# A top-k attention block with a squared-ReLU feed-forward: first scores in parts, fewer reciprocals, other warming products, a new plan

## The chip, the cores and the metric

The program runs on one core of a Trainium2 chip. The core has five instruction streams, which run side by side and meet only at semaphores: TensorE (PE, matrix products; its weight loads are shown apart, as PEld), VectorE (DVE), ScalarE (ACT), GpSimd (POOL) and SyncE (SP, which issues most DMAs). The metric is the device time of one execution in microseconds (us), lower is better.

## The reference, cut to what matters

```python
# q, k, v: [8, 8, 576, 64] f32; w_in: [512, 2048], w_out: [2048, 512]
scores = (1 / sqrt(64)) * q @ k.T                   # per batch and head: 576 x 576
kth = the 32nd largest of each row
scores = where(scores >= kth, scores, -1e9)
attn = softmax(scores)
x = (attn @ v), heads side by side, as [4608, 512]
out = (max(x @ w_in, 0) ** 2) @ w_out
```

## The kernel before, in words

Two heads of one batch are a pair; a pair's 576 queries are cut into four blocks of 128 and one of 64 (two pairs share the blocks of 64). A block of one pair is a group, 144 groups in all, numbered n in the order of work. Every group goes through the same steps:

- Loads: `load_pair` brings q and k of the pair (three DMAs each) and v. `load_first` does it for the first pair alone, in smaller pieces: half of k over ACT's queue, the rest over SP's, q in two row blocks and a remainder.
- Transposes on PE (line 714) into two PSUM banks, copied to SBUF by ACT and DVE (lines 772 to 783, 848 to 850).
- `score`: four f32 products of PE (line 711; each shows as two passes), named by RUNS: run 0 is head 0, columns 384 to 575; run 1 head 1, columns 192 to 575; run 2 head 0, columns 0 to 383; run 3 head 1, columns 0 to 191. Head 0 lies in partitions 0 to 63, head 1 in 64 to 127. Runs 0 and 3 write the same PSUM bank, so run 3 waits on a semaphore, `fence`, that run 0 raises. One set of three banks holds the scores, so the next group's scores wait until these are read.
- `copied` (line 895): ACT copies the scores to SBUF. For the first two groups (`early`) a first quarter of the columns goes first and the rest after DVE's three folds.
- `top_k`: DVE folds the quarters of a row on each other (line 966, maxima), either itself or with POOL (lines 983 and 986, or 961 with a DMA of line 971 called edge) forms the rest, and finds the 32nd largest by rounds of the eight largest (lines 1019, 1024, 1034) and their replacement (line 1031). The third round's replacement is done by DVE (line 999) or by signs on ACT (line 1005) and a product on POOL (line 1009); the string SIGNS chooses, m or s, for each group.
- `attend`: ACT forms the mask (line 1053), PE transposes the scores with the mask added (line 714 and `steep_bf`), ACT takes the exponential (line 1110), PE multiplies with v (`fetch`).
- `gather` and `collect`: the sums are copied; for two pairs at a time DVE takes the reciprocals of the row sums (line 1184), POOL multiplies (line 1186), and a transposing DMA (line 1201) writes the result as the feed-forward's input.
- `feed`: PE multiplies with w_in, ACT takes the ReLU, POOL or ACT squares, PE multiplies with w_out (line 711).

The order of all this is planned in Python when the program is built. Every operation has a planned duration; the plan simulates the engines and gives each engine a fixed order. The strings in ORDERS hold that order (each character picks the next operation out of those left). On the chip an engine runs its instructions in that order and waits on semaphores, not on the plan's times. Besides, the planner puts in products that compute nothing needed, to keep PE at work: warming products at the start (`times`, 128 x 512 on `ones_bf`) and spare ones later. A warming product is placed only if PE is free at that planned time, the next planned operation is not delayed and one of two PSUM banks is free; otherwise it is dropped.

Of the kernel before, what the change touches and what calls it, by code (L numbers as in the profile page):

```python
# [448 lines left out]
def bass_top_k_attn__then__act_relu_squared_kernel(  # L449
# [24 lines left out]
    def sb(name, shape, dt=FP32, n=None):  # L474
        if n is None:
# [12 lines left out]
    SIGNS = "sssmmsmsssmmsmsmmsmssmsmmsmsmssmmmssssmsmmsmmsmmsmsmsmmsmsmsmsmmssmmsssmsmssmmsmmmsmmsssmmsmmmssmsmmsmsmssmsmsmmsmsmmmmmmmmmssmmmssmsmsmssmmmmmm"  # L488
# [7 lines left out]
    WARM = 6.4  # L496
    HOT = 6
# [8 lines left out]
            "222020343040402504406700Q561ON61714N6M1561W6H15T61Q71b461ZY75166AABB86618576B8A8158861968AC961EK6DHF176FAC6617"  # L506
            "5qs1q617B5A7186788991996DAC1C6B81b75A1X6BAD1B571868L56A1UAHHR1GGDHH519C8D6C1B9335491555867761686666156C8CABD77"
            "6196~118D8199568716=71;AAEEJJ1UU6MM15EQUUQ15655I9BA9148995744851AAgCf1CEONGF1IWIEGED1HQQIPP1QQLTT4C11J3251211G"
            "388964D1F7742G1444F55A14455A14D6AAB173445A51D597691666461kl61B5666615599666B1A7775716Z68J15C7S61CPA6861649UU1H"
            "HE9F1EGGE4FF17D8A46414925A55E155AA55155A67C18C96677415~119671A699771646A;A16CC61EEEJJO1NPPMRR14K5444454F4413F3"  # L510
            "E4554SCST1FCOFNKJR1GHEOE1JCDIL1HHMOHN4MMOOCG121H34J3275111864FB421G6444G1B4444551C5665A1D6665A1D56B6A1A7764AA1"
            "688DD61KQKP61IOOM1QmQN4544514544644FF464S4D1RHDQO1DMLHRHH1ELDFCD1HHOJHH4LMC165614M3111Q28I751P21233Q1K3333331O"
            "3333M122333775H14I633D1F393A616AF377421FB55551H445555144475o5914757Bh1H9f7694E1NEFE3DV1DEJDDPLL1CCDCCDCCPCG1OG"
# [16 lines left out]
        "dve": (  # L530
            "00330L0LJ0330FTSGFG0ENFM0LEEJ330GRIBQFH0LF4481BU8E10011O04c8J7I5667F7D1661L0MM98Z94AH5A8F1160O8M9L68WWJ7811046"
            "5N555962250EE4E54B55M9K2K2Y1H2G52F4D5552523102G3D4364OBO181702244DFD44524L270J7G86E2D8RQ24294281860GFG14656191"
            "812I2H05235354A951L160J51X442436C491A81706HH22T5465B52A2430H7G3F4U45R4B6PO59bA9A92H923S1SE26BN5A6992I231R735DB"
            "6A5990G9A41D1S029A6A5797A16E71705A5A67K7I777262660A9AM9K99958992C20A01888L88J8944171606A9A589867G7177D1S0C9C9C"
            "L9KD9YJ5H2H230Q4CPDN5BZ555252GS14555AB608481616062A9P999N995I19190D24BBB5A658297270A39999595972H20063CC3549547"
            "7576165155088888888574171D0D3A59A9AM9A91A1302C75A59758L72J25054E64C6Q5B62A273136F4E4D65CN5M6282712G354CD4OO5AB"
            "M2K281266SF78OEC3B2AAHCB2F55C2C1ALA0A5G8FF5E8EQDP27C2D09II96A5F8RQ92D2600J7I75G6678D1B1N0999KIAA558181A0AN5N89"
            "8J6872T2F0D5C55BAB658F2827B1B39OAONB9Ca5201G048D1D3D5E61841605E3CD65N59A5A82G2F0E3T74BB4AMAA5J0I191G22S03B5A4A"
            "4B64151D0C6C3AB4949J4A1615C70BA2AO9A9A551G1808C4C5ABMA597H88298C2RC309AM6A8B85HGA7272615805I7I6G6F76D871Q1A0OM"
            "A57JA7BG46171P0B5MB95867881ED1D05NC695898A9D2C2R0359898985727E2E61B5BA69999A5292C1B3A069NA85781H15064C5B5B5562"  # L540
            "J2505EF64C4C659N92K2J162G6U04RED555144171504ED23RB6AN4AM9188Y1Y0HkF8EF3D2N5B525K27370D3CDC6B5C552G7D271A028888"
            "889481C1A01847777476I171E03C55A6A95861J61G04EE64P5BN5556272505ED4CC4M5B59A929231C629A9A9A9B9294DCD2B129996L58J"
            "JJ79H2H2F1P4NDM66KCB62B291D3BC4ABA6A0HGA242C60AAAAAA59AA52C2C1A0A2MA8A8479F16170B1B9B9LB55716170D5BCBP5A59L752"
            "72G04FR4F65OEB652CJ2313U4CE4B4A5NA2829J12F9E2S4QD6BN2692416HG4T06RE74O5bAMM5952U2460Q74D5MB5AA55A828D2B13A9A96"
            "A95F82200584777M777K716180D2D4BC6ABK591G1906C72BAMBLCKA3C924F230B4MALL59JA9BV9GA52C2B1A2AJ9IBY595927C26186N770"
            "YL66HJ8GA1G1H03LB5AJ69FH518140O9BMDML958572G2E076C6AMA69IJ2Y2G1406CC56578572J2G0F54DD054548414F1E04D63A394M989"
            "8A17180B1B1QB9PBM6516170HFS84F8CM4BL5242303FT546DA59BK2J2B1X6014C164Q7dO884713140G3E3QD4C6cC5A59AA161D0DA29B68"
            "KB57G292D0PC4NC5MC5567268251S59A9A9L9K55II2I27R1EFE476B7J051E1706A3999999AFA52D2D029B9B557A7A26261658677706666"
            "667171AA0999O9598J95H191F0D4PC5NCBML65KJ92A2T04D50N6NAAMA1I1AV13EF30EC75EA575B2E2D06BB6B89A9B92E2813BA0A9OA955"
            "K9729728D16C76B9KB7CI272W1DED50Q4CAC5MLA2KJ2819GR2G7D8N72D6L28G28H8184AO6ABLDK7383G2FF9E0D5C6B662992516B7ABBB6"  # L550
            "AOB0962I2I6617FD8C6C6A6920J1H034EEE5E5Q5O6292381HH93W95D5D6B62A241485F5F6667A89N3087879798E281ABO6979L89K8AU83"
            "02C0B5AMBABAC5A2D2C1C309A969572G2G0V5D6DCD6BN7B62B271GF4VFE5EQ66E029425308EE4DD6NC7C6A6262EE175B6BACALCBD3B02D"
# [167 lines left out]
    def build(full, weights, pl):  # L720
# [137 lines left out]
        def score(gi, qks, tg, st, early=False):  # L858
# [39 lines left out]
            if early:  # L898
                return ss, [copied(0, QUART)], lambda after: copied(QUART, S, after=after)
# [720 lines left out]
```

## Time and profile before

| | us |
|---|---|
| median of 3 runs | 748.02 |
| lowest, highest | 747.33, 749.09 |
| the profiled execution | 746.35 |
| its span (first to last instruction) | 744.5 |

| engine | busy us | share of the span | instructions |
|---|---|---|---|
| PE | 702.2 | 94% | 10653 |
| DVE | 724.7 | 97% | 3426 |
| ACT | 707.5 | 95% | 1225 |
| POOL | 692.5 | 93% | 525 |

All four engines are busy nearly all the time. The profile also has a chain of waits, which is followed back from the last instruction: at each step it goes to what released the instruction, or to the one before it on its engine. Matmuls overlap, so a sum of their durations can be longer than the stretch they lie in.

### The profile page before, as it was taken

The page shows a single profiled execution, that of the slowest core. Times are in us where ns is not written, and L with a number is a line of the kernel's source. Part 1 is how long each engine was busy: PE and PEld are TensorE (multiplying, and loading weights), DVE is VectorE, ACT ScalarE, POOL GpSimd, SP SyncE. Part 2 cuts the span into 40 slices and gives each one's busy share as a digit, 9 for nine tenths or more (in the row PEclk, how much of TensorE's full clock was granted, in tenths as well). Part 3 has the DMA queues.
Part 4 walks back from the last instruction along what each step waited for, and adds up shares of the span by engine and source line. Part 5 has one row for each costly group of instructions (what it writes and reads, how often), then busy time and mean ns, then how long its engine had stood idle before and what let it go on. Part 6 is the DMA issues. An engine that isn't in the chain of part 4 may idle for free.

```text
span 744.5 us, 27576 instructions
## 1 busy us (share of the span) xinstructions
PE 702.2 (94%) x10653; PEld 524.3 (70%) x10653; DVE 724.7 (97%) x3426; ACT 707.5 (95%) x1225; POOL 692.5 (93%) x525
## 2 busy tenths in 40 slices
PE   8788898989989899999999999999999999999998
PEld 4566766767768667766667777777676777777776
DVE  4999999999999999999999999999999999999996
ACT  2799999999999999999999999999999999999994
POOL 3699999999999999999999999999999999999972
PEclk9999999999999999999999999999999999999999
DMA  7569763225424523436343363423654135321111
GB/s 167 152 179 217 152 175 85 68 70 111 104 59 94 126 69 78 94 83 123 82 103 72 81 149 71 88 64 94 113 120 101 46 88 100 80 72 42 62 36 63
DMA packets 191368, 73.21 MB, mean 98 GB/s; under 512 B 139520, under 2 KB 182528, under 8 KB 191232
## 3 DMA queue, kind: packets, MB, share of 16 engines
q1 hardware_dynamic: 182880, 66.59, 36.0%
q0 software_dynamic: 7392, 4.13, 4.6%
q8 instruction: 84, 1.38, 0.8%
q10 hardware_dynamic: 960, 0.69, 0.3%
q14 instruction: 52, 0.43, 0.2%
HBM read 40.83 MB, written 13.57 MB: 73 GB/s over the span
## 4 chain that ended last, share of the span: by engine, by line
DVE 60%; PE 20%; ACT 9%; POOL 8%; issue 2%; DMA 1%; POOLq 0%
PE ps L711 17%; DVE f L966 13%; DVE c L1024 13%; DVE f L1031 12%; DVE kth L1034 9%; DVE f L1019 9%; PE ps L714 4%; DVE f L999 3%; POOL f L961 3%; POOL u L961 3%; ACT w L1053 2%; ACT s L895 2%; ACT p L1110 1%; POOL g L1247 1%; ACT g L1232 1%
## 5 line engine op out<-in xcount | busy, mean ns | idle before, releaser
L961 POOL TENSOR_TENSOR u<-s,f 128x864 int32<-128x864 int32 x140 | 239.6, 1714 | 5.2 <-DVE f L966 5.1
L961 POOL TENSOR_TENSOR f<-u,f 128x864 int32<-128x864 int32 x140 | 239.3, 1713 | 4.4 <-DMA f<-s 1.4
L1053 ACT ACTIVATE w<-s,kth 128x576 bf16<-128x576 f32 x286 | 220.7, 799 | 2.0 <-DVE kth L1034 1.3
L1024 DVE MAX8 c<-f 128x8 f32<-128x92 f32 (+2 forms) x864 | 207.8, 266 | 0.2
L711 PE MATMUL ps<-qk 64*128 64x384 f32 (+3 forms) x1280 | 179.2, 428 | 11.9 <-DVE f L966 10.2
L895 ACT COPY s<-ps 128x1152 f32<-128x1152 f32 (+2 forms) x146 | 164.2, 1125 | 13.0 <-PE ps L711 9.9
L1110 ACT ACTIVATE p<-ps 128x1152 bf16<-128x1152 f32 x144 | 165.8, 1151 | 1.3 <-PE ps L711 1.1
L711 PEld LDWEIGHTS ps<-qk 64*128 64x128 f32 (+1 forms) x1280 | 130.2, 175 | 45.9 <-DVE f L966 28.4
L711 PE MATMUL ps<-wo,g 128*128 128x512 bf16 (+1 forms) x592 | 146.7, 375 | 1.6 <-ACT av L1177 1.2
L1031 DVE MATCH_REPLACE8 f<-c,f 128x112 f32<-128x112 f32 (+1 forms) x576 | 140.6, 247 | 0.0
L711 PE MATMUL ps<-xt,win 128*128 128x256 bf16 (+1 forms) x1280 | 134.5, 252 | 1.6 <-ACT qk L848 0.5
L1034 DVE MAX8 kth<-f 128x8 f32<-128x296 f32 x288 | 128.4, 453 | 1.2 <-POOL f L1009 0.9
L966 DVE TENSOR_TENSOR f<-ps,f 128x288 f32<-128x288 f32 x288 | 126.9, 440 | 0.5
L1019 DVE MAX8 f<-f 128x8 f32<-128x288 f32 x288 | 124.9, 444 | 0.1
L714 PEld LDWEIGHTS ps<-ident,s 64*128 64x128 f32 x2592 | 98.1, 139 | 36.1 <-ACT w L1053 17.1
L714 PE MATMUL ps<-ident,s 64*128 64x64 f32 x2592 | 110.8, 227 | 9.8 <-ACT w L1053 7.6
L711 PEld LDWEIGHTS ps<-xt,win 128*128 128x128 bf16 x1280 | 98.6, 98 | 26.0 <-issue 4.8
L1247 POOL TENSOR_TENSOR g<-g 128x1024 bf16<-128x1024 bf16 x58 | 109.6, 1892 | 4.1 <-DMA xt<-x 3.2
L1232 ACT ACTIVATE g<-ps 128x512 bf16<-128x512 f32 x140 | 84.3, 619 | 1.4 <-PE ps L711 0.6
L711 PEld LDWEIGHTS ps<-wo,g 128*128 128x128 bf16 x592 | 48.7, 98 | 46.1 <-issue 5.1
L711 PEld LDWEIGHTS ps<-vb,p 128*128 128x128 bf16 (+1 forms) x1600 | 54.4, 100 | 23.4 <-issue 4.0
L711 PE MATMUL ps<-vb,p 128*128 128x65 bf16 (+1 forms) x1600 | 63.2, 195 | 4.3 <-ACT g L1232 2.3
(91 smaller groups left out, 803.6 us busy)
## 6 DMA issues: line engine op xcount, KB each, us to landing
f<-s SPq DMA_DIRECT2D x140, 144.0 KB, 2.3
out_dram<-o SPq DMA_DIRECT2D x32, 256.0 KB, 2.4
rk<-in_k_dram SPq DMA_DIRECT2D x63, 128.0 KB, 2.5
rq<-in_q_dram SPq DMA_DIRECT2D x62, 128.0 KB, 2.6
g<-in_moe_w_out_dram SPq DMA_DIRECT2D x16, 256.0 KB, 3.7
vd<-in_v_dram POOLq DMA_DIRECT2D x14, 288.0 KB, 4.8
g<-in_moe_w_in_dram SPq DMA_DIRECT2D x14, 256.0 KB, 3.8
vb<-vd SPq DMA_DIRECT2D x56, 64.0 KB, 2.4
```

Of the source, the lines that this page charges most:

```text
L711: return pe.matmul(o, l, r, start=start, stop=stop, skip_group_check=True)
L714: return pe.matmul(o, i, ident, is_transpose=True, skip_group_check=True, **kw)
L895: return pl.op("act", .14 + 2 * (c1 - c0) / 1200, (tg - LEAD + 1), lambda: act.copy(at(st)[:, :, c0:c1], two(banks(ss)[:, FIRST_AT + c0:], ...
L961: return pl.op("gp", dur, prio, lambda: gp.tensor_tensor(o().bitcast(I32), x().bitcast(I32), y().bitcast(I32), op), **kw)
L966: return dve(.36, lambda: vec.tensor_tensor(o(), two(banks(ss)[:, FIRST_AT + c:], SECOND, QUART), x(), ALU.max), r=[ss], **kw)
L1019: prev[i] = [dve(.065 + HALF / 960, lambda i=i: vec.max(at(f)[:, i, M:M + 8], at(f)[:, i, z:z + HALF]), after=prev[i] + [low], hold=[f])]
L1024: lambda i=i, t=t, c0=c0, c1=c1: vec.max(eighth(t, i), at(f)[:, i, c0:c1]),
L1031: lambda i=i, t=t, c0=c0, c1=c1: vec.match_replace(at(f)[:, i, c0:c1], eighth(t, i), at(f)[:, i, c0:c1], NEG), hold=[f])]
L1034: ks.append(chain(kth, i, prev[i], .065 + (8 + HALF) / 960, lambda i=i: vec.max(eighth(kth, i), at(f)[:, i, z + HALF:M + 8]), hold=[f]))
L1053: masks[i:] = [pl.op("act", .764, (tw + .8 * i), lambda i=i: act.activation(at(wt)[:, i, :], at(st)[:, i, 0:S], ACTF.Relu, bias=kth[:, i, ...
L1110: return act.activation(at(pt)[:, :, :].rearrange("p c (h q) -> p h c q", h=2), bass.AP(x.tensor, x.offset, [x.ap[0], [APART, 2], [64, 9], ...
L1247: pl.op("gp", 1.851, (tf + lag + 1), lambda g=g: gp.tensor_tensor(at(g)[:, :], at(g)[:, :], at(g)[:, :], ALU.mult), u=[g])
```

## The change

- Groups 0 and 1: the four runs of the scores become three operations of PE, in the order run 2, then runs 0 and 3, then run 1, each planned at 0.37 us; the copy of the first quarter becomes two instructions, one for each head, behind the first and the second of these.
- Where a row block of 128 is collected alone (batch 6, and two of the four blocks of batch 7), all four pairs are collected at once instead of two and two: one reciprocal and one product on POOL, and two transposing DMAs one after the other.
- Warming products: eight single ones at the start instead of seven; then two single ones and a triple at planned times of their own instead of one block of six.
- The planned durations of DMAs: the first pieces longer, the others shorter.
- Group 56: signs on ACT instead of DVE's replacement.
- All five order strings are written anew (left out of the diff below).

```diff
-    SIGNS = "sssmmsmsssmmsmsmmsmssmsmmsmsmssmmmssssmsmmsmmsmmsmsmsmmsmsmsmsmmssmmsssmsmssmmsmmmsmmsssmmsmmmssmsmmsmsmssmsmsmmsmsmmmmmmmmmssmmmssmsmsmssmmmmmm"
+    SIGNS = "sssmmsmsssmmsmsmmsmssmsmmsmsmssmmmssssmsmmsmmsmmsmsmsmmsssmsmsmmssmmsssmsmssmmsmmmsmmsssmmsmmmssmsmmsmsmssmsmsmmsmsmmmmmmmmmssmmmssmsmsmssmmmmmm"
...
-    WARM = 6.4
-    HOT = 6
+    WARM = 7.4
...
-            pl.op("sp", 3.3, base - 82, start(nc.scalar, lambda: part(rk, k, 0, 0, 4),
+            pl.op("sp", 4.05, base - 82, start(nc.scalar, lambda: part(rk, k, 0, 0, 4),
...
-            rows.append(pl.op("sp", 2.6, base - 79.5, start(nc.sync, lambda: (at(rq)[:, 1, :, :], both[1])), hold=[rq],
+            rows.append(pl.op("sp", 3.9, base - 79.5, start(nc.sync, lambda: (at(rq)[:, 1, :, :], both[1])), hold=[rq],
...
-                pl.op("sp", 4.0, (base - 80), load(rq, q), w=[rq], take=[rq], sem=slot_sem, ndma=3,
+                pl.op("sp", 3.0, (base - 80), load(rq, q), w=[rq], take=[rq], sem=slot_sem, ndma=3,
...
-            pl.op("pe", 1.075 if gi != Z else 1.04, (tg - LEAD), scores if gi != Z else scores_z, r=qu, w=[ss],
-                  take=[ss, st], tiled=True)
+            def first_of(h, after):
+                return pl.op("act", .25, (tg - LEAD + 1), lambda: act.copy(
+                    at(st)[:, h, 0:QUART], banks(ss)[:, FIRST_AT + SECOND * h:][:, 0:QUART]), hold=[ss], w=[st], after=[after])
...
             if early:
-                return ss, [copied(0, QUART)], lambda after: copied(QUART, S, after=after)
+                parts, quarters = [], []
+                def some(runs):
+                    o, x = banks(ss), at(qks[0])
+                    for i in runs:
+                        h, to, c0, n_ = RUNS[i]
+                        if i == 3:
+                            pe.wait_ge(fence, fences[0])
+                        ins = mm(o[:, to:to + n_], x[64 * h:64 * h + 64, 128 * gi:128 * gi + 128],
+                                 x[64 * h:64 * h + 64, S + c0:S + c0 + n_], i < 3)
+                        if i == 0:
+                            fences[0] += 1
+                            ins.then_inc(fence, 1)
+                    return ins
+                for i, (dur, runs) in enumerate(((.37, [2]), (.37, [0, 3]), (.37, [1]))):
+                    parts.append(pl.op("pe", dur, (tg - LEAD + .01 * i), lambda runs=runs: some(runs), r=qu, w=[ss],
+                                       take=[ss, st] if i == 0 else [], order=parts[-1:], tiled=True))
+                    if i < 2:
+                        quarters.append(first_of(i, parts[-1]))
+                return ss, quarters, lambda after: copied(QUART, S, after=after)
...
-                    edge = pl.op("sp", 3.4, tg - MT - 1, lambda: [nc.sync.dma_start(
+                    edge = pl.op("sp", 2.2, tg - MT - 1, lambda: [nc.sync.dma_start(
...
-            if rows:
-                _, u0, n_, (xt, col, first), hp = rows[0]
-                ops += 2 * [pl.op("sp", 3.1, (tt + 5), lambda u0=u0, n_=n_, xt=xt, col=col, hp=hp: [nc.sync.dma_start_transpose(
+            for k_ in range(0, len(rows), 2):
+                _, u0, n_, (xt, col, first), hp = rows[k_]
+                ops += 2 * [pl.op("sp", 2.3, (tt + 5), lambda u0=u0, n_=n_, xt=xt, col=col, hp=hp: [nc.sync.dma_start_transpose(
...
+                    four = gi != Z and len(js) == 1 and i < len(CHUNKS) - 2
+                    full_ = hp % (4 if four else 2) == (3 if four else 1) or CHUNKS[i] is CHUNKS[-1] and hp == NHP - 2 if gi != Z else (last or b in ZF) and hp
...
-        times = [(COLD * i, COLD) for i in range(int(WARM / COLD)) if COLD * i < 2.8]
-        times += [(WARM, COLD * HOT)]
+        times = [(COLD * i, COLD) for i in range(int(WARM / COLD)) if COLD * i < 3.1]
+        times += [(4.97, COLD), (6.9, COLD), (7.93, 3 * COLD)]
```

## Rows read from the trace of the kernel before

**Rows 1.** Stretches: length; PE, PEld, DVE, ACT, POOL busy (instructions); granted clock; DMA
```profile
0.00:17.10 17.10, 13.73 (x57) 7.04 (x58) 6.51 (x23) 5.10 (x11) 5.88 (x35) 1.00 0.71 168
17.10:300.00 282.90, 257.53 (x3897) 191.94 (x3896) 282.46 (x1330) 272.65 (x471) 270.86 (x196) 1.00 0.49 117
...
345.00:362.00 17.00, 16.31 (x245) 11.74 (x239) 16.13 (x77) 16.39 (x29) 15.55 (x14) 1.00 0.62 124
362.00:728.70 366.70, 360.15 (x5648) 272.64 (x5649) 365.65 (x1757) 361.61 (x624) 352.64 (x250) 1.00 0.36 84
728.70:744.50 15.80, 12.76 (x166) 10.05 (x163) 8.92 (x30) 6.88 (x15) 3.52 (x3) 1.00 0.11 41
```
**Rows 2.** Chain of waits, 600 to 720 us, shares by engine and line
```profile
by line: PE ps L711 78.5%; PE ps L714 16.6%; ACT s L895 1.8%; ACT p L1110 1.2%; ACT w L1053 0.7%; issue 0.6%; ACT g L1232 0.5%; ACT av L1177 0.1%
```
**Rows 3.** Timeline of the start: start, length, engine, line, count, idle time before and its releaser
```profile
1.07 3.17 PE L711 MATMUL ps<-ones_bf 128*128 128x512 bf16 x7 [1.07 <-DVE ones_bf L1409]
5.14 1.39 PE L714 MATMUL ps<-ident,rk 128*128 128x128 f32 x5 [0.90 <-POOL vb L1429]
7.40 2.29 PE L711 MATMUL ps<-qk 64*128 64x192 f32 x8 [0.47 <-ACT qk L772]
9.89 2.44 PE L711 MATMUL ps<-ones_bf 128*128 128x512 bf16 x6
10.17 0.46 DVE L966 TENSOR_TENSOR f<-ps,s 128x288 f32<-128x288 f32 x1 [3.21 <-ACT s L895]
11.64 0.88 ACT L895 COPY s<-ps 128x864 f32<-128x864 f32 x1 [1.51 <-DVE f L966]
12.74 1.24 PE L711 MATMUL ps<-qk 64*128 64x192 f32 x8 [0.41 <-ACT qk L779]
14.03 0.40 ACT L895 COPY s<-ps 128x288 f32<-128x288 f32 x1 [1.34 <-PE ps L711]
14.46 0.46 DVE L966 TENSOR_TENSOR f<-ps,s 128x288 f32<-128x288 f32 x1 [0.40 <-ACT s L895]
14.81 0.86 PE L714 MATMUL ps<-ident,rq 128*128 128x128 f32 x5
...
20.11 0.44 DVE L966 TENSOR_TENSOR f<-ps,s 128x288 f32<-128x288 f32 x1
```
**Rows 4.** PE's groups by shape, 7.3 to 9.9 us: busy us, mean ns
```profile
L711 PE MATMUL ps<-qk 64*128 64x384 f32 x4 | 2.3, 884 | 0.0
L711 PE MATMUL ps<-qk 64*128 64x192 f32 x4 | 1.9, 564 | 0.5 <-ACT qk L772 0.5
```
**Rows 5.** The same, 12.7 to 14.0 us
```profile
L711 PE MATMUL ps<-qk 64*128 64x384 f32 x4 | 1.2, 508 | 0.0
L711 PE MATMUL ps<-qk 64*128 64x192 f32 x4 | 1.1, 349 | 0.4 <-ACT qk L779 0.4
```
**Rows 6.** Timeline of DVE around two of its short instructions
```profile
701.11 0.16 DVE L1184 RECIPROCAL rzall<-av 128x4 f32<-128x4 f32 x1
701.19 0.44 DVE L1034 MAX8 kth<-f 128x8 f32<-128x296 f32 x1
...
704.13 0.07 DVE L999 MATCH_VALUE_LOAD f<-c,f 128x8 f32 x1
...
704.40 0.08 DVE L999 MATCH_VALUE_LOAD f<-c,f 128x8 f32 x1
```
**Rows 7.** Groups of the signs, whole span: busy us, mean ns
```profile
L1005 ACT ACTIVATE g<-f,c 128x147 f32<-128x147 f32 x128 | 55.1, 445 | 2.4 <-DVE c L1024 1.7 <-POOL f L1009 0.6
L1009 POOL TENSOR_TENSOR f<-f,g 128x294 f32<-128x294 f32 x64 | 47.1, 737 | 10.5 <-ACT g L1005 9.9
```
**Rows 8.** Chain of waits, 260 to 310 us, shares
```profile
by line: POOL f L961 19.4%; POOL u L961 19.2%; POOL g L1247 14.9%; DVE c L1024 7.5%; DVE f L966 7.3%; DVE kth L1034 6.8%; DVE f L1031 6.6%; issue 6.6%; DVE f L1019 4.3%; POOL f L1009 2.8%; POOL x L1186 2.5%; DVE f L999 2.3%; POOLq L438 0.1%
```
**Rows 9.** The edge transfers (line 971), and POOL behind the late one
```profile
DMA to landing us min/median/max: 2.1/2.3/6.0
...
355.31 1.71 POOL L961 TENSOR_TENSOR f<-u,f 128x864 int32<-128x864 int32 x1 [1.37 <-DMA f<-s]
```

More of the change, by code (lines that the diff above doesn't have):

```diff
@@ L510, in bass_top_k_attn__then__act_relu_squared_kernel @@
[L510 to L513, printed above, removed]
@@ L569, in bass_top_k_attn__then__act_relu_squared_kernel @@
+            "1AC03C734B329297T07679PO95007060240066407673A491B33BC3B32B2A8AQ018O68M10706G32527005366AA15C377CD523A6B2A2A706"
+            "918605502460142013423001341020403411230012010"
         ),
@@ L817, in load_pair @@
             else:
[L818 removed]
+                pl.op("sp", 3.0, (base - 80), load(rq, q), w=[rq], take=[rq], sem=slot_sem, ndma=3,
                       bw=BW * 1.9)
[L820 removed]
+                pl.op("sp", 3.0, (base - 79.9), load(rk, k), w=[rk], take=[rk], sem=slot_sem, ndma=3, bw=BW * 1.9)
             qk, vb = tile("qk"), tile("vb")
             if b:
[L823 removed]
+                pl.op("sp", 2.6, (base - VA), loadv, w=[vb], take=[vb], sem=slot_sem, ndma=4, bw=2.41,
                       after=[] if full else [landed[b, hp // 2]])
@@ L896, in copied @@
                     at(st)[:, :, c0:c1], two(banks(ss)[:, FIRST_AT + c0:], SECOND, c1 - c0)), r=[ss], w=[st], **kw)
+            def first_of(h, after):
+                return pl.op("act", .25, (tg - LEAD + 1), lambda: act.copy(
+                    at(st)[:, h, 0:QUART], banks(ss)[:, FIRST_AT + SECOND * h:][:, 0:QUART]), hold=[ss], w=[st], after=[after])
             if early:
-                return ss, [copied(0, QUART)], lambda after: copied(QUART, S, after=after)
+                parts, quarters = [], []
[17 more added lines that the diff above has]
+                return ss, quarters, lambda after: copied(QUART, S, after=after)
+            pl.op("pe", 1.075 if gi != Z else 1.04, (tg - LEAD), scores if gi != Z else scores_z, r=qu, w=[ss],
+                  take=[ss, st], tiled=True)
             cp = [copied(0, S)]
@@ L1197, in collect @@
             rows = [p for p in got["parts"] if p[0] != Z]
-            if rows:
-                _, u0, n_, (xt, col, first), hp = rows[0]
-                assert [p[1:3] + (p[4],) for p in rows] == [(u0, n_, hp), (u0 + n_, n_, hp + 1)]
-                ops += 2 * [pl.op("sp", 3.1, (tt + 5), lambda u0=u0, n_=n_, xt=xt, col=col, hp=hp: [nc.sync.dma_start_transpose(
+            for k_ in range(0, len(rows), 2):
+                _, u0, n_, (xt, col, first), hp = rows[k_]
+                assert [p[1:3] + (p[4],) for p in rows[k_:k_ + 2]] == [(u0, n_, hp), (u0 + n_, n_, hp + 1)]
+                ops += 2 * [pl.op("sp", 2.3, (tt + 5), lambda u0=u0, n_=n_, xt=xt, col=col, hp=hp: [nc.sync.dma_start_transpose(
                     at(xt)[:, hp:hp + 2, col:col + 64 * n_].rearrange("p a (i q) -> p (a i) q", q=P) if n_ == 4 else
                     at(xt)[:, hp:hp + 2, col:col + 64 * n_], flat(xr, u0, 2 * n_))], r=[xr], w=[xt],
-                    take=[xt] if first else [], ndma=1, bw=.32 * n_, sem=lambda o: f"x{xr.slot}")]
+                    take=[xt] if first else [], ndma=1, bw=.32 * n_, sem=lambda o, k_=k_: f"{'xy'[k_ // 2]}{xr.slot}")]
             for gi, u0, n_, (xt, col, first), hp in got["parts"]:
@@ L1385, in build @@
                     gather(got, gi, groups, parts, hp, tt)
-                    full_ = hp % 2 or CHUNKS[i] is CHUNKS[-1] and hp == NHP - 2 if gi != Z else (last or b in ZF) and hp
+                    four = gi != Z and len(js) == 1 and i < len(CHUNKS) - 2
+                    full_ = hp % (4 if four else 2) == (3 if four else 1) or CHUNKS[i] is CHUNKS[-1] and hp == NHP - 2 if gi != Z else (last or b in ZF) and hp
                     if not full_:
```

104 lines of the change are left out of this document (52 added, 52 removed).

## The prediction, made before the changed kernel ran

> **What bounds the kernel now.** I read the table of stretches first, because VectorE (DVE) is 97% busy over the whole span and that average hides where it is not. The table shows one engine without slack: DVE is busy 6.51 us of the first 17.10, then almost all of every stretch up to 728.7 us (365.65 of 366.70 in the longest), and 8.92 of the last 15.80 [rows 1]. So the time is a start of 10.6 us in which DVE waits, some 711 us of DVE work with 2.4 us of holes, and a tail. 0.87 us of those holes lie in 17 us around 350.
>
> The chain of waits then says which engine sets the end: from 600 us on it runs over TensorE (PE) alone, 95% of it [rows 2]. PE has a backlog there, so a DVE saving after 600 buys little, while a delay at the start is handed on to all that follows: DVE has no free stretch in which to catch up.
>
> Third comes the timeline of the first 15 us [rows 3]. The products that warm PE take 3.17 us for seven of 512 columns, 0.45 us each, which is the 1.2 GHz level. The first group's scores (eight passes) start at 7.40 and take 2.29 us; the second group's, after six more products, take 1.24 us, the 2.4 GHz level. The granted clock of the table reads 1.00 in all stretches and shows nothing of this; the passes' own durations do, 884 and 564 ns in the first group against 508 and 349 in the second [rows 4, 5]. After the scores ScalarE (ACT) copies a quarter, and DVE's first fold starts at 10.17. For the second group it is 12.74, 14.03 (the copy, 0.40 us) and 14.46, where DVE had stood idle for 0.40 us.
>
> **The change part by part: scores in three parts.** A group's scores are two heads, which lie in the two halves of PE's rows. In the second group the eight passes add up to 4 x 508 + 4 x 349 = 3428 ns, yet the block is over in 1.24 us [rows 3, 5]: the heads run side by side. The old order alternates them (head 0, 1, 0, 1). The new one is run 2 (head 0), run 0 (head 0), a wait on the fence that run 0 raises, run 3 (head 1), run 1 (head 1). Two runs of one head follow each other on the same rows, and the wait stands in PE's queue ahead of all that head 1 does. So the side-by-side part is lost. What is won is the quarter copy, now two instructions that run while later parts are computed. The first fold reads columns of runs 0 and 1, so it needs the last part.
>
> The trace has no such sequence. Below it can't cost less than the old block with the copy hidden: 7.40 + 2.29 + 0.05 = 9.74 for the first fold, 0.43 earlier. Above it is twice the block: 4.58 us at the low clock (fold at 12.01, 1.84 later), 2.48 at the high one (9.91, 0.26 earlier). For the first group I take the middle of the two serial values, 3.53 us, as if the clock rose on the way: fold at 10.96, 0.79 later.
>
> For the second group the clock is up. The copy of its queries now stands ahead of the rest copy on ACT, so its scores can start as that copy ends (11.64 + 0.88) instead of at 12.74: 12.57. Then 2.48 + 0.03 gives 15.08 where 14.46 was, 0.62 later. If the heads did overlap, DVE would still have its own work to do until 0.40 us before that. Behind the second group's folds 14 DVE operations of the first two groups stand ahead of the third group's first fold (16 before, when it came at 20.11 without a wait), so the third group adds nothing. Start in all: 0.79 + 0.62 = 1.41 later, bounds 0.83 earlier and 2.46 later.
>
> **Warming products.** Eight single ones instead of seven ahead of the transposes, then single ones and a triple between transposes, scores and the second block; thirteen in all if every one is placed, and thirteen before. The one more at the front lies in PE's idle stretch from 4.24 to 5.14 [rows 3] and costs nothing. The one meant to stand between transposes and scores needs one of two PSUM banks, and both hold the transposed k and q at that time; the planner drops a product that finds none within 0.3 us of its plan. I count it as not placed. If it is, it lies in the 0.47 us for which PE waits there [rows 3], and nearly hides.
>
> The Trainium skill, page "TensorE: Matmul & The Clock Gate", section "Part 1: The HAM clock gate", says that what decides the clock runs free of the kernel's start, so that the same kernel has more slow matmuls in one execution than in the next. No run here shows it; by it the first group would be at 2.48 in some executions and at 4.58 in others, 2.10 us apart. The three times shown differ by 1.76.
>
> **Less DVE work.** Group 56 changes from wiping on DVE to signs on ACT. A wipe is two instructions from 704.13 to the next at 704.40, 0.27 us; two make 0.54 [rows 6]. ACT gets two looks, 0.45 us and the reading of a count each, and GpSimd (POOL) a multiplication of 0.74 [rows 7]. The group is ranked near 300 us, where the chain runs 59% over POOL [rows 8], so I take 0; bounds 0.54 less and 0.74 more. Reciprocals: twelve of four columns become six of eight. From 701.11 to the next instruction at 701.19 one takes 0.08 us [rows 6]: six fall away, 0.48 at most, and I take 0.30, as the six that stay are twice as wide. They belong to the last two batches, mostly in PE's stretch: 0.10 less of the time; bounds 0.48 less and, as four rows' worth is now multiplied and turned at once after the fourth pair, 0.5 more if PE's backlog did not cover it. It does for the stretch [rows 2].
>
> **DMAs and orders planned anew.** No DMA is added or removed, apart from moved ones: the second q block is issued behind the second pair's k (its turn on PE comes only after the scores, so it is covered), and a weight block goes ahead of two loads. The planned edge transfer falls from 3.4 to 2.2; the trace has a landing of 2.3 in the median and 6.0 at most, and the late one at 349 us held POOL for 1.37 [rows 9] and made the 0.87 us hole in DVE [rows 1]. A new order will not have the same collision: I take 0.87 less. Bounds: all holes of DVE closed, 2.4 less; two more such collisions, 1.74 more.
>
> **Sum.** 1.41 - 0.10 - 0.87 = 0.44 later. The profiled execution took 746.35 us (744.5 of span and 1.85 around it); it would be 746.79. It lies 1.67 under the median of the runs shown, so I add the 0.44 to that: 748.02 + 0.44 = 748.5.
>
> **The rivals.** Faster: the eighth product and the denser stretch bring the clock up before the scores. For it: one stretch of products from 9.89 on was enough. Against it: seven from 1.07 were not. Then five transposes take 0.86 us as at 14.81 instead of 1.39, 0.53 earlier, the first fold is at 7.40 - 0.53 + 2.48 + 0.03 = 9.38 (0.79 earlier), the second 0.17 earlier; with the wipes' 0.54, the 0.10 and the 0.87 it is 1.68 less: 746.3.
>
> Slower: the serial first group stays at the low clock throughout, with one half of the rows at a time, and no hole closes: 1.84 + 0.62 - 0.10 = 2.36 more, 750.4. It decides from a start 1.6 us later without the hole's return. For it: in this trace the clock was low through all of the first group's scores. Against it: work almost without a break from 7.40 had brought the clock up by 12.74, and the serial block would end at 11.98.
>
> Slower too: orders planned on shorter transfers leave POOL waiting for edges. Two more collisions: 1.74 + 1.41 - 0.10 = 3.05 more, 751.1. For it: landings up to 6.0; against it: one in 140 edges was waited for.
>
> That the change doesn't do what it says: the three parts take the time of two heads in a row, not 0.37 each as planned; this is my forecast, and its opposite (heads overlap) would end with the faster rival.
>
> **How the numbers follow.** Forecast 0.42, faster rival 0.27, cold first group 0.21, late edges 0.10. A measurement of this kernel can tell 0.2%, 1.5 us, from no change: the forecast lies inside, from 746.5 to 749.5, and that is its own range; the others lie outside. So faster 0.27, same 0.42, slower 0.31. The range reaches from 745.7, past the faster rival, to 750.8, past the cold one.
>
> **What would show it.** In the new trace: the two first score blocks. If the runs of head 1 start after those of head 0 end and a block takes 2.4 us or more at the high clock, the serial reading is right; at 1.3 it is wrong. The first and second folds at 10.96 and about 15.9. Whether a product stands between transposes and scores, and at what durations the passes run. DVE's busy time 0.84 us lower, its holes after 17 us under 2. The chain after 600 us still on PE. A first fold before 9.5 or a chain that leaves PE after 600 would make the forecast wrong.

## The result, and the profile after

The changed kernel takes 758.74 us in the median (755.86 to 759.51, 4 runs) against 747.67 of the kernel before beside it: a ratio of 1.0139 [1.0107, 1.0172], 1.4% slower. The forecast was 748.5, its range ended at 750.8. The profiled execution took 758.03 us with a span of 756.1, 11.6 longer than the profiled one of before. The ratios here and below leave out three executions that ran slow at a mean granted clock of 0.56 to 0.85 (one of f3_narrow, two of the kernel before).

The stretches of the kernel after, with the columns of [rows 1]:
```profile
0.00:27.00 27.00, 23.41 (x60) 11.79 (x60) 9.74 (x35) 7.68 (x15) 7.51 (x37) 1.00 0.48 117
27.00:262.00 235.00, 208.80 (x3232) 158.20 (x3248) 234.02 (x1101) 227.27 (x393) 222.75 (x166) 1.00 0.52 124
262.00:276.00 14.00, 13.27 (x202) 10.96 (x201) 11.56 (x57) 11.41 (x21) 12.13 (x8) 1.00 0.34 82
276.00:376.00 100.00, 95.07 (x1451) 71.45 (x1460) 99.93 (x474) 98.99 (x180) 98.14 (x70) 1.00 0.39 88
376.00:390.00 14.00, 13.09 (x160) 9.14 (x160) 12.58 (x60) 12.38 (x21) 12.56 (x9) 1.00 0.44 97
390.00:740.30 350.30, 337.89 (x5373) 259.94 (x5415) 348.25 (x1665) 343.99 (x591) 334.08 (x232) 1.00 0.35 83
```
DVE (the fourth figure) stands still for 17.3 us of the first 27, where it was 10.6 us of the first 17.1 in [rows 1]: 6.7 us lost before the work is in step. Then 2.4 us are lost between 262 and 276, and 1.4 between 376 and 390. The stretches between these are as full as they were; after 390 DVE is idle for 2.05 us, where it was 1.05 in about as long a stretch after 362 [rows 1]. How far the one instruction that ends every half of a group (the MAX8 into kth, 288 of them) lags in each profiled execution says the same, in us from the start of the span (in the kernel after 0.5 of the 11.6 us come only behind the 288th):

| kernel | 1st | 97th | 121st | 145th | 288th | span |
|---|---|---|---|---|---|---|
| before | 24.96 | 261.0 | 319.4 | 379.1 | 728.2 | 744.5 |
| after | 32.12 | 268.3 | 328.6 | 389.3 | 739.4 | 756.1 |
| lag | 7.2 | 7.3 | 9.2 | 10.2 | 11.1 | 11.6 |

**The start.** The timeline of the kernel after, the columns as in [rows 3]:
```profile
7.69 4.63 PE L710 MATMUL ps<-qk 64*128 64x384 f32 x8 [0.47 <-ACT qk L771]
9.37 0.28 ACT L896 COPY s<-ps 128x144 f32<-128x144 f32 x1 [1.74 <-PE ps L710]
11.07 0.28 ACT L896 COPY s<-ps 128x144 f32<-128x144 f32 x1 [1.42 <-PE ps L710]
12.43 0.46 DVE L989 TENSOR_TENSOR f<-ps,s 128x288 f32<-128x288 f32 x1 [5.18 <-PE ps L710]
13.18 1.49 PE L710 MATMUL ps<-ones_bf 128*128 128x512 bf16 x3
14.84 4.62 PE L710 MATMUL ps<-qk 64*128 64x384 f32 x8 [0.17 <-ACT s L892]
19.57 0.46 DVE L989 TENSOR_TENSOR f<-ps,s 128x288 f32<-128x288 f32 x1 [3.11 <-PE ps L710]
22.99 2.29 PE L710 MATMUL ps<-qk 64*128 64x192 f32 x8
26.48 0.46 DVE L989 TENSOR_TENSOR f<-ps,s 128x288 f32<-128x288 f32 x1 [1.72 <-ACT s L892]
28.29 1.24 PE L710 MATMUL ps<-qk 64*128 64x192 f32 x8
```
A block of eight passes takes 4.63 and 4.62 us where it took 2.29 and 1.24 [rows 3]. The third group's block has its heads side by side and still takes 2.29; the first in 1.24 us is the fourth group's, at 28.29. The passes of one head and of the other, taken from two windows of that timeline, show why:
```profile
7.69 2.29 PE L710 MATMUL ps<-qk 64*128 64x384 f32 x4 [0.47 <-ACT qk L771]
10.03 2.28 PE L710 MATMUL ps<-qk 64*128 64x192 f32 x4
```
Head 0's four passes come first and head 1's start when they are over. The wait on the fence alone would enforce this, since run 3 is the first of head 1 and waits for run 0, the last of head 0. No run has this order without the wait, so what the shared rows add to it is not shown.

The groups by shape inside the second block answer to [rows 5]; they stand where the first group's stood [rows 4]:
```profile
L710 PE MATMUL ps<-qk 64*128 64x384 f32 x4 | 3.1, 884 | 0.2 <-ACT s L892 0.2
L710 PE MATMUL ps<-qk 64*128 64x192 f32 x4 | 1.8, 564 | 0.1
```
884 and 564 ns are the 1.2 GHz level. The trace's record of the granted clock has its first rise at 26.5 us, and at 11.9 in the kernel before; the table's clock column knows nothing of the time before the first record and shows 1.00 there. The other three executions of the kernel after have no trace, but their mean granted clock over the span is 0.984 to 0.989. That is some 17 to 24 us at the lower level behind a first rise (an estimate: twice the missing share of their spans). In the 70 executions of the kernel before that the ratios of the experiments count, the mean is 0.995 or more. So a long stretch at the lower level is not a matter of the one trace.

**266 us.** The timelines of PE, ACT and DVE:
```profile
266.30 2.84 PE L710 MATMUL ps<-ident_bf 128*128 128x128 bf16 x48
269.07 1.24 PE L710 MATMUL ps<-qk 64*128 64x192 f32 x8
270.36 1.12 ACT L892 COPY s<-ps 128x1152 f32<-128x1152 f32 x1 [2.59 <-PE ps L710]
271.51 0.46 DVE L989 TENSOR_TENSOR f<-ps,s 128x288 f32<-128x288 f32 x1 [2.44 <-ACT s L892]
```
48 spare passes (16 products of the planner, three passes each; the longest row in the kernel before is 15 passes, 1.00 us) stand in PE's queue ahead of a group's scores. ACT waits for the scores, and DVE for ACT.

**Later.** The chain from 600 to 720 us was PE's for 95% [rows 2]; now PE has 62%, and the rest is mixed:
```profile
by line: PE ps L710 50.0%; PE ps L713 12.1%; ACT s L892 5.3%; ACT p L1133 5.2%; ACT w L1076 5.1%; POOL g L1270 4.6%; POOL u L984 3.6%; POOL f L984 2.8%; ACT g L1255 2.3%; DMA xt<-x 2.0%; issue 1.9%; POOL x L1209 1.7%; POOL f L1032 1.1%; SPq
```
The edge transfers land as before (2.2/2.3/6.3 us against 2.1/2.3/6.0 [rows 9]).

### The profile page after: what moved, and what is told of

Same layout as the page of the kernel before. It is cut to its first block, busy times and chain, and to the rows that moved or that the text cites. A ratio compares the mean times of both kernels' runs of the same rounds, so it can differ in the third digit from the quotient of the medians.

```text
span 756.1 us, 27588 instructions
## 1 busy us (share of the span) xinstructions
PE 704.1 (93%) x10627; PEld 531.6 (70%) x10700; DVE 724.9 (96%) x3416; ACT 708.6 (94%) x1231; POOL 690.7 (91%) x520
## 4 chain that ended last, share of the span: by engine, by line
DVE 39%; ACT 27%; PE 20%; POOL 9%; issue 3%; DMA 2%; SPq 0%; POOLq 0%; DVEq 0%; ACTq 0%
PE ps L710 16%; DVE f L989 9%; DVE c L1047 9%; DVE f L1054 7%; ACT w L1076 7%; ACT s L892 6%; DVE kth L1057 6%; ACT p L1133 6%; DVE f L1042 6%; PE ps L713 4%; POOL f L984 4%; POOL u L984 3%; ACT g L1255 2%; DVE f L1022 2%; ACT g L1028 2%
## 5 line engine op out<-in xcount | busy, mean ns | idle before, releaser
L1047 DVE MAX8 c<-f 128x8 f32<-128x92 f32 (+2 forms) x864 | 212.2, 270 | 0.2
L710 PE MATMUL ps<-qk 64*128 64x384 f32 (+3 forms) x1280 | 186.1, 431 | 13.3 <-DVE f L989 11.7
L892 ACT COPY s<-ps 128x1152 f32<-128x1152 f32 (+1 forms) x144 | 162.7, 1130 | 13.7 <-PE ps L710 12.3
L710 PEld LDWEIGHTS ps<-qk 64*128 64x128 f32 (+1 forms) x1280 | 133.2, 177 | 49.7 <-DVE f L989 30.7
L1054 DVE MATCH_REPLACE8 f<-c,f 128x112 f32<-128x112 f32 (+1 forms) x576 | 142.4, 251 | 0.0
L710 PE MATMUL ps<-wo,g 128*128 128x512 bf16 (+1 forms) x519 | 130.2, 373 | 11.8 <-issue 6.5
L1042 DVE MAX8 f<-f 128x8 f32<-128x288 f32 x288 | 126.5, 448 | 0.1
L989 DVE TENSOR_TENSOR f<-ps,s 128x288 f32<-128x288 f32 x144 | 64.0, 444 | 14.4 <-PE ps L710 8.3
```

The costliest lines, as they stand in the source:

```text
L710: return pe.matmul(o, l, r, start=start, stop=stop, skip_group_check=True)
L892: return pl.op("act", .14 + 2 * (c1 - c0) / 1200, (tg - LEAD + 1), lambda: act.copy(at(st)[:, :, c0:c1], two(banks(ss)[:, FIRST_AT + c0:], ...
L989: return dve(.36, lambda: vec.tensor_tensor(o(), two(banks(ss)[:, FIRST_AT + c:], SECOND, QUART), x(), ALU.max), r=[ss], **kw)
L1042: prev[i] = [dve(.065 + HALF / 960, lambda i=i: vec.max(at(f)[:, i, M:M + 8], at(f)[:, i, z:z + HALF]), after=prev[i] + [low], hold=[f])]
L1047: lambda i=i, t=t, c0=c0, c1=c1: vec.max(eighth(t, i), at(f)[:, i, c0:c1]),
L1054: lambda i=i, t=t, c0=c0, c1=c1: vec.match_replace(at(f)[:, i, c0:c1], eighth(t, i), at(f)[:, i, c0:c1], NEG), hold=[f])]
```

## The experiments

Theory P: two runs of one head in a row are worked one behind the other, and PE with half of its rows at work does not get its clock up; that is the start's loss. Theory S: the row of spares is the loss at 266 us. Rivals: W, the other warming products keep the clock down; O, the new orders themselves; C, the cut into parts as such.

**Undo one part, do one part.** e1_whole, on the changed kernel:
```
-                for i, (dur, runs) in enumerate(((.37, [2]), (.37, [0, 3]), (.37, [1]))):
-                    parts.append(pl.op("pe", dur, ..., lambda runs=runs: some(runs), ...
+                parts = [pl.op("pe", 1.075, (tg - LEAD), scores, r=qu, w=[ss], take=[ss, st], tiled=True)]
+                quarters = [copied(0, QUART)]
...
```


> The changed kernel with one edit: the first two groups' scores again as one block, heads in turn, with the one copy of both heads' first quarter; warming products, orders, reciprocals and transfers stay as changed. Theory P (the parts set one head's products behind the other's, and half-wide products in a row keep the clock at its lower level): the first block takes about 2.3 us and not 4.6, the clock rises by 15 us instead of 26.5, the first kth MAX8 comes near 25 to 27 us instead of 32.1, and the time falls by 5 to 7 us, to about 752 us. Rival W (the other warming products keep the clock down, the parts cost only their own passes): the clock still rises after 20 us, the second block still runs at the lower level, and the time falls by 2 to 4.5 us.

749.61 us, 1.0041 [1.0024, 1.0058] of the kernel before, where the changed kernel stood at 1.0139: 7.3 of the 10.4 us are gone by the ratios, a little more than P had said, and well above the 2 to 4.5 of W. The profiled run was the slowest of the ten (754.03); its clock went up and down (below), and its first kth came at 27.31.

e2_parts is the reverse, on the kernel before: the three parts and the head-by-head copies go in, and the orders stay.
```
+                for i, (dur, runs) in enumerate(((.37, [2]), (.37, [0, 3]), (.37, [1]))):
+                    parts.append(pl.op("pe", dur, ...
...
-    HOT = 6
+    HOT = 5
```


> The kernel before with one edit: the first two groups' scores in the three parts of the change and the first quarter copied head by head; orders as before, the warming products as before but five instead of six behind the first block. Theory P: the two blocks take 4.6 us each or 4.6 and 2.5, the clock rises later than 11.9 us, the first kth MAX8 comes 4 to 7 us later than 25.0, the time rises by 4 to 7 us to 752 to 755 us. Rival W: the clock rises at about 14 us with the products still there, the second block runs in 2.5 us, and the time rises by 2 to 3.5 us.

753.39 us, 1.0071 [1.0047, 1.0094]. Its timeline of PE:
```profile
7.61 4.63 PE L713 MATMUL ps<-qk 64*128 64x384 f32 x8 [0.47 <-ACT qk L774]
12.44 2.34 PE L713 MATMUL ps<-ones_bf 128*128 128x512 bf16 x5
14.93 4.62 PE L713 MATMUL ps<-qk 64*128 64x384 f32 x8
23.88 1.24 PE L713 MATMUL ps<-qk 64*128 64x192 f32 x8
```
The five products, 0.47 us each, are still at the lower level, as is the second block; the rise is at 23.3, the first kth at 31.20, 6.2 late. So the parts alone, with the old products and the old orders, bring nearly all of the start's 7.2, and by the 97th kth the lag is 7.2 as well.

e4_warm gives the kernel before the changed one's products:
```
-        times = [(COLD * i, COLD) for i in range(int(WARM / COLD)) if COLD * i < 2.8]
-        times += [(WARM, COLD * HOT)]
+        times = [(COLD * i, COLD) for i in range(int(7.4 / COLD)) if COLD * i < 3.1]
+        times += [(4.97, COLD), (6.9, COLD), (7.93, 3 * COLD)]
```


> The kernel before with one edit: the changed kernel's warming products instead of its own (8 at first, then single ones instead of the six behind the first block); the scores stay whole. Theory P: whole blocks alone suffice or cost one stretch at the lower level: the clock rises at latest by 16 us and the time rises by 0 to 1.5 us. Rival W: without the six the clock rises after 20 us, the second and third group's scores run at the lower level, and the time rises by 3 to 5 us to 751 or 752.

747.35 us, 1.0011 [0.9990, 1.0031]: no difference. On these orders seven of the eight are placed at the start and three where six stood; the clock rises at 11.8 all the same. W falls for whole blocks; e2_parts, with the old products, shows the loss without the new ones.

**The row of spares.** e3_spares, on the changed kernel:
```
-                if e == "pe" and spare and free(...
+                if e == "pe" and spare and not all(x.fill for x in order[e][-2:]) and free(...
```


> The changed kernel with one edit: no more than two spare products of the planner in a row (of its 46 it keeps 24; the 16 planned ones that run as 48 passes at 266.3 us become 2). Theory S (these passes hold up the scores behind them): the scores that started at 269.1 start near 266.7, DVE's hole of 2.4 us at 271.5 goes to under 0.5, and the time falls by 2 to 3 us to about 756. Rival O (the new order of SP, a load of v ahead of the edge copy, makes the hole and the spares only fill it): the hole stays over 1.5 us and the time falls by under 1 us.

754.76 us, 1.0103 [1.0068, 1.0137], by the ratios 2.7 us less than the changed kernel, though the two intervals overlap; the trace decides. In its timelines the passes before the scores are six, and DVE's fold has no idle time before it:
```profile
266.42 0.50 PE L710 MATMUL ps<-ident_bf 128*128 128x128 bf16 x6
266.85 1.24 PE L710 MATMUL ps<-qk 64*128 64x192 f32 x8
269.29 0.46 DVE L989 TENSOR_TENSOR f<-ps,s 128x288 f32<-128x288 f32 x1
```
The lag behind the kernel before is 7.4 us at the 97th kth and 7.0 at the 121st, where it grew from 7.3 to 9.2 after the change. That is 2.3 us for S. O's reading of this hole falls: SP's order, with a load of v ahead of an edge copy there, is unchanged, and the hole is gone.

**Both.** e5_both has the edits of e1_whole and e3_spares.

> The changed kernel with two edits: whole score blocks for the first two groups, and no more than two spare products in a row. Theory P with S (the parts and the row of spares are all of the loss that counts): what e1_whole and e3_spares gave back adds up, 9.1 and 4.0 us less what both share, so 746.5 to 748.5 us, even with the kernel before. Rival O (the new orders themselves leave holes that stay: in them a load of v on SP stands ahead of edge copies at several places): DVE idles over 2 us more between 250 and 700 us than before, and the time stays at 749.5 to 751.

749.57 us, 1.0047 [1.0028, 1.0067]: a miss for P with S by 1 us, no better than e1_whole, and inside the time that O gave. The profiled execution lags by 1.3 us at the first kth, 0.2 at the 121st and 2.3 at the 288th: some 2 us are lost after 330 us (1.25 of idle DVE at 376, where before had 0.87 at 361; the rest in small ones). Between 250 and 700 us DVE is idle for 2.34 us and was for 0.94, so 1.4 more where O asked for over 2. The next run has the same orders and loses the same 2.0 us between the 121st and the 288th kth (0.7 to 2.7), yet its median is even with the kernel before. So the traces show a loss with the new orders there; that it is a loss in the total is not shown.

**Heads side by side.** e7_side keeps parts and head-by-head copies and changes which passes stand together (with e3's edit):
```
-                for i, (dur, runs) in enumerate(((.37, [2]), (.37, [0, 3]), (.37, [1]))):
+                front = pl.op("pe", .7, (tg - LEAD), lambda: some([3, 2]), ...
+                quarters = [first_of(0, front)]
+                back = pl.op("pe", .375, (tg - LEAD + .01), lambda: some([1, 0]), ...
+                quarters.append(first_of(1, back))
...
```


> The changed kernel with no more than two spares in a row, and the first two groups' scores in two parts in place of three, each with one pass of either head, so that the heads stand side by side: first head 0's columns 0 to 383 with head 1's 0 to 191, then head 1's 192 to 575 with head 0's 384 to 575; the copies of the first quarter head by head as in the change. Theory P (it is the heads one behind the other that cost, not the cut into parts): the block takes 2.3 to 2.6 us, the clock rises as early as in e5_both, and the time is within 1 us of e5_both. Rival C (the cut itself, more waits and a copy more, costs): the first fold comes over 0.7 us later than in e5_both and the time is 2 us or more above it.

747.57 us, 1.0004 [0.9987, 1.0020]. The start, PE and DVE:
```profile
7.20 2.29 PE L715 MATMUL ps<-qk 64*128 64x192 f32 x8 [0.47 <-ACT qk L776]
12.25 2.29 PE L715 MATMUL ps<-qk 64*128 64x192 f32 x8 [0.41 <-ACT s L897]
18.07 1.24 PE L715 MATMUL ps<-qk 64*128 64x192 f32 x8 [0.30 <-ACT qk L854]
9.84 0.46 DVE L992 TENSOR_TENSOR f<-ps,s 128x288 f32<-128x288 f32 x1 [3.09 <-ACT s L901]
14.90 0.46 DVE L992 TENSOR_TENSOR f<-ps,s 128x288 f32<-128x288 f32 x1 [0.31 <-ACT s L901]
```
The block takes 2.29 us, as a whole one does. The fence is still there, raised by run 3 and awaited by run 0, but no longer stands between the heads. C falls, for two parts at least: it was not the cut, only which passes stand next to each other. Some 10 us lie between this kernel and the changed one, and two edits. That it is 2 us below e5_both was not expected.

**One group at a time**, on the kernel before: e8_second and e9_first put the parts in under a condition.
```
-            if early:
+            if early and n_th == 1:      # e9_first: n_th == 0, and HOT = 5
```


> The kernel before with the three parts for the second group alone; the first group's block and the six products behind it stay. The term of my sum taken by itself: with the clock up at 11.9 us the second block takes 2.5 us instead of 1.24 and the time rises by 0.4 to 0.9 us. Rival F (half-wide passes pull the clock down again): the clock falls after this block, later blocks take 2.3 us, and the time rises by 2 to 4 us.

750.49 us, 1.0057 [1.0035, 1.0079], and yet not what F says. PE's timeline, and from the view of one line the branches that close the program (least, median and longest ns):
```profile
7.05 1.66 PE L713 MATMUL ps<-qk 64*128 64x192 f32 x8 [0.47 <-ACT qk L774]
11.76 2.52 PE L713 MATMUL ps<-qk 64*128 64x384 f32 x8 [0.29 <-ACT qk L781]
17.30 1.24 PE L713 MATMUL ps<-qk 64*128 64x192 f32 x8
L1588 PEldq COMPARE_BRANCH  x1: 4526/4526/4526, 743.2 to 743.2; - x1
```
With the clock up the serial block takes 2.52 us (I had 2.48), and the clock stays up. The 288th kth comes 0.66 later than before, the span ends 3.6 later: PE's closing branch took 4.53 us here and 0.41 to 0.42 in the other profiles. So neither the total nor the lag is the price of the parts: the first block had the clock up for part of its time and was 0.63 us shorter, and the first kth comes at 24.92, no later than before. The other three executions took 750.3 to 751.1, so the long branch may belong to this kernel and not to this one execution; no run shows why it is long.

> The kernel before with the three parts for the first group alone (five products behind it instead of six); the second group's block is whole. Theory P: the first block takes 4.6 us, the first fold comes 2 us later, and the clock does not rise until the second block, with both heads side by side, has run: it takes 2.3 us and not 1.24; the time rises by 3 to 4.5 us. Rival B (each group's parts cost only their own passes, and the clock rises with the products behind the first block): the second block takes 1.24 us and the time rises by 1.8 to 2.6 us.

750.89 us, 1.0062 [1.0040, 1.0083], 3.3 us more by the medians and 4.6 by the ratio, as P said or just above. PE's timeline:
```profile
6.83 4.63 PE L713 MATMUL ps<-qk 64*128 64x384 f32 x8 [0.47 <-ACT qk L774]
11.66 2.34 PE L713 MATMUL ps<-ones_bf 128*128 128x512 bf16 x5
14.14 2.29 PE L713 MATMUL ps<-qk 64*128 64x192 f32 x8
20.34 1.24 PE L713 MATMUL ps<-qk 64*128 64x192 f32 x8
```
The serial first block and five products behind it leave the clock down; the whole second block pays 2.29 for it.

**Is it the rows?** f3_narrow, on the kernel before:
```
+            k_ = P // 2 if x < 7 else P
-   [mm(bank(t), ones_bf[:, :], ones_bf[:, :].unsqueeze(1).broadcast_to([P, 4, P]), True) ...
+   [mm(bank(t), ones_bf[0:k_, :], ones_bf[0:k_, :].unsqueeze(1).broadcast_to([k_, 4, P]), True) ...
```


> The kernel before with its thirteen first warming products on 64 of the 128 rows instead of all: the same count, columns and time on PE; the scores stay whole. Theory H (a pass on half of the rows does less for the clock than a full one, which is why the parts kept it down): the clock rises later than 14 us, the second block takes 2.3 us, and the time rises by 1 to 3 us. Rival T (it is PE's busy time that counts, whatever the rows, and the parts cost only by their double time): the clock rises at about 11.9 us as before and the time stays within 0.5 us.

748.89 us in the median of nine executions, 1.0029 [1.0012, 1.0046]. The timeline of PE:
```profile
1.07 3.16 PE L711 MATMUL ps<-ones_bf 64*128 64x512 bf16 x7 [1.07 <-DVE ones_bf L1409]
7.32 2.29 PE L711 MATMUL ps<-qk 64*128 64x192 f32 x8 [0.47 <-ACT qk L772]
9.95 2.74 PE L711 MATMUL ps<-ones_bf 64*128 64x512 bf16 x6
12.67 2.29 PE L711 MATMUL ps<-qk 64*128 64x192 f32 x8
19.42 1.24 PE L711 MATMUL ps<-qk 64*128 64x192 f32 x8
```
Up to 11.9 us PE is as long at work as in [rows 3], pass for pass; only the rows are halved. The time is 2.2 us above the kernel before by the ratio, where T allowed 0.5: T falls. The trace is as H says, with the rise at 17.1 us and not 11.9 and the second block at the lower level. But one trace can't carry this part: e5_both and e7_side, with full rows and the heads side by side, have their first rise at 17.0 and 16.6. H rests on the time of nine executions and is supported, not settled.

**A better version?** Three tries: e10_before_side (e7's two parts on the kernel before), f1_early (nine first products instead of seven, on the kernel before) and f2_side_early (e7_side with nine instead of eight).
```
-   n=max(1, round(dur / COLD)): [mm(
+   n=max(1, round(dur / COLD)) + 2 * (x == 0): [mm(      # f2_side_early: + 1 *
```


> The kernel before with the first two groups' scores in two parts that keep the heads side by side (as in e7_side) and the first quarter copied head by head; nothing else. Theory P (only the heads one behind the other cost): each block still takes 2.3 us at the lower clock level, the copy of head 0 runs under the second part, and the first two folds come 0.1 to 0.3 us earlier: 747.0 to 747.7 us, no difference that can be told. Rival C (the cut costs): 1 to 2 us slower.

> The kernel before with nine warming products ahead of the first transposes instead of seven, so that PE's idle time of 0.3 to 1.25 us there is filled. If the clock rises before the first scores (it showed its upper level from 3.8 and 4.3 us in two profiled runs, and the first block took 2.1 and 1.7 us in them), the transposes and the first block lose up to 1.7 us: 745.7 to 747. Rival: the clock rises at 11.9 us as before and the products only delay the transposes when k lands early: 747.4 to 748.

> e7_side (heads side by side, no more than two spares in a row) with nine products at the start instead of eight. It is the version of the change with its two losses taken out; e7_side stood at 1.0004 [0.9987, 1.002] of the kernel before. If the extra product brings the clock up early: 746 to 747. If not: 747 to 748.

746.92 us, 0.9998 [0.9983, 1.0012]; 747.62, 1.0001 [0.9987, 1.0015]; 746.95, 1.0001 [0.9987, 1.0015]: none differs from the kernel before. f2_side_early's profiled execution did have the clock up from 5.3 us on:
```profile
6.67 1.24 PE L715 MATMUL ps<-qk 64*128 64x192 f32 x8 [0.47 <-ACT qk L776]
10.68 1.24 PE L715 MATMUL ps<-qk 64*128 64x192 f32 x8 [1.41 <-ACT s L897]
19.11 2.29 PE L715 MATMUL ps<-qk 64*128 64x192 f32 x8
```
Its first fold came at 8.27, its first kth at 23.96; then the record has the clock down from 19.0 to 22.4. One product more does not settle it: f1_early's profile shows a first block of 2.29 behind nine.

## Why the prediction was wrong, step by step

**The step that failed** is "For the second group the clock is up", and with it "I take the middle of the two serial values, 3.53 us, as if the clock rose on the way". I had taken the time at which the clock rose before as given and put the new passes beside it; with the parts in, it came later (26.5 us for 11.9, and 23.3 in e2_parts, which changes little else). For the first group I had 0.79; the block of 4.63 instead of 3.53 adds 1.1, and k's later transposes 0.3 (5.43 for 5.14): the first fold is 2.26 late. For the second I had 0.62, and 4.62 us for 2.48: the second fold is 5.11 late (19.57 for 14.46). "So the third group adds nothing" fell too: its block runs in 2.29 with the clock still down, DVE waits 1.72 for it, and the first kth is 7.16 late. 1.41 was forecast for the start, with 2.46 as upper bound; that bound had 4.58 us for the first block and, for the second, the upper level again.

**Right**: heads behind each other and not side by side (4.63 = 2 x 2.29 + 0.05), the quarter copies hidden (9.37 and 11.07, both under later parts), the eighth product at the front without cost, the one between transposes and scores not placed. That DVE can't catch up held too: the lag is 7.2 us at the first kth and 7.3 at the 97th. e8_second shows that 2.48 was right where the clock is up.

**The rival "cold first group"** (750.4) had the mechanism and named what should decide it: one half of the rows at a time. Against it I set "work almost without a break from 7.40 had brought the clock up by 12.74": that work was full rows or two heads at once. The low clock was priced for one group, not for all that follows until it rises. e9_first comes nearest to that rival: 750.89, with the low clock in the second block too.

**No term at all** stood for the planner's spare products: 2.3 us (e3_spares). I had costed "orders planned anew" by the transfers alone; the operations that a plan inserts by itself where it sees PE idle were not looked for.

**Holes.** The 0.87 that I took off was not won: in the new trace DVE idles 1.25 at 385. With the new orders some 2 us are lost between the 121st and the 288th kth in the kernel after, e5_both and e7_side alike. Which of the moved instructions bring it was not tried; nor were the collecting of four pairs at once and group 56 undone alone.

**The chain after 600 us** left PE (62% for 95%), which I had named as a sign that the forecast is wrong. The forecast counted on a backlog of PE there. It is gone with the new orders and not with the late start: e2_parts, with the old orders and the start as late, still has PE at 90%, and e7_side, with the new ones, at 64%.

**Less DVE work** came as written: 37 reciprocals for 43, 7.0 us for 7.7; two wipes fewer, 158 for 160. DVE's total stayed (724.9 for 724.7 us), since its long instructions ran some ns longer (the kth MAX8 457 for 453 in the mean; 453 to 467 over all these profiles). The late edges (751.1) did not happen: POOL waited for four, 1.5 us together.

**Open** is why e5_both and e7_side stand 2 us apart in their medians. Their profiled spans, 747.3 and 747.7, do not show it: the profiled execution is the fastest of five in the one and the slowest of ten in the other. In both the first rise is near 17 us there.

## What to carry to other kernels

Before cutting a block of matmuls into parts, look whether its passes overlap on different rows: where the sum of the passes is more than the block's length, the order of the passes, and of the waits between them, is part of its speed. A warm-up is not a date in the trace: it changes with the passes that stand before it and with the execution (first rise at 3.8 us in e1_whole's trace and at 17.0 in e5_both's, with the same operations on PE up to there). Replace these passes and the price can be the lower level for all groups until the next rise; judge it by several executions. After planning anew, list what the planner inserted by itself, and what stands in the queue behind it.

## What the runs showed of the hardware

With both blocks one head at a time, the traces have the clock's first rise at 23.3 (e2_parts), 26.5 (after) and 30.8 us (e3_spares); with the first block alone at 16.7 (e9_first). In the nine kernels with a side-by-side first block and full-row products it lies between 3.8 (e1_whole) and 17.0 us (e5_both). So two such blocks stand clear of the rest, one does not. Half-row products alone had it at 17.1 us (f3_narrow) and cost 2.2 us over nine executions.

The Trainium skill, page "TensorE: Matmul & The Clock Gate", section "Part 1: The HAM clock gate", has the clock follow how busy PE was of late. In the kernel after, PE was at work for 11.43 of the 11.77 us from 7.69 on and stayed at the lower level; in the kernel before it was at work for the 4.47 us from 7.40 to the rise. So the profile's busy time alone doesn't tell when the clock rises here. That the rows at work matter is the reading that f3_narrow supports; it is not the whole account, since e1_whole, with whole blocks, has a stretch of 13.6 us at the lower level too (below).

The same kernel's executions differ by the clock's course at the start. The granted clock of stretches of e1_whole, the column before the last two:
```profile
7.00:9.20 2.20, 2.17 (x9) 1.62 (x9) 0.00 (x0) 0.00 (x0) 0.00 (x0) 0.55 0.79 173
12.00:13.30 1.30, 1.26 (x9) 1.01 (x10) 1.24 (x2) 0.00 (x0) 1.30 (x2) 1.00 0.61 137
17.50:31.10 13.60, 12.39 (x44) 7.28 (x41) 10.74 (x36) 5.95 (x14) 1.43 (x2) 0.50 0.45 108
```
The record has the clock up at 3.8 us, down at 7.2, up at 10.6, and down again from 17.5 to 31.1; this run took 754.03, the nine others 748.55 to 752.06. e2_parts' eight runs lie in two bunches, three at 750.0 to 750.2 and five at 753.3 to 754.3. The same section of the Trainium skill says that what decides the clock runs free of the kernel's start. Bunches like these agree, though only one run of each kernel has a trace.

PE's closing branch took 4.53 us in one kernel (e8_second) and 0.41 to 0.42 in the others; it was over at 747.77, when the last of the other engines had been done since 744.97.
